# Attention, a Mish layer and a gated layer in one kernel: the written-out order planned anew with two times for each kind of transfer

## The chip, the core and the metric

The kernel runs on one core of a Trainium2 chip. The metric is the device time of one execution in microseconds. Three runs of the kernel before took 959.82, 963.29 and 963.5 us; the median is 963.29 us.

## What is computed

Inputs and outputs are float32. Three layers follow each other, on 4 batches of 576 tokens with 8 heads of 64 columns:

```python
# 1. attention, blocks of 64 tokens, a block sees itself and the blocks before it
scores = where(block_i >= block_j, (q @ k.T) / 8, -1e9)
attn = softmax(scores);  x = (attn @ v)            # 2304 tokens x 512
# 2. Mish layer, 512 -> 2048 -> 512
h = x @ w_in;  g = h * tanh(log1p(exp(min(h, 20))));  x = g @ w_out
# 3. RMS norm and gated layer, 512 -> 1536 -> 512
xn = x / sqrt(mean(x * x) + 1e-6) * rms_g
out = (silu(xn @ w_gate) * (xn @ w_val)) @ w_out2
```

## The kernel before, in words

**Arithmetic.** Most products are made of three float16 products of high and low halves ("hi" and "lo"), so each tile is first scaled and split by ScalarE, VectorE or GpSimd. The first 256 tokens go through the Mish layer in float32 (N32 = 1), and the first batch has float32 queries and keys (B32 = 1). Weights arrive as 64-bit words that VectorE turns into float32 in three instructions a tile (`to_f32`, L578, L586 and L606, where L606 is the last one).

**Tiling.** Attention goes batch by batch through five query tiles of 128 rows (the last has 64). For each head, or pair of heads, TensorE makes scores `s` (L978 to L1001), VectorE the row maximum `mx` (L1018), ScalarE the exponential `e` (L1043), and the probabilities are split and transposed into `pt`, in the first query tiles on TensorE (L1068, L1089), from the fifth query tile of batch 0 on by a DMA transpose (L1134). TensorE then multiplies `pt` by `v` into `x` (L1147, L1155), and VectorE scales that into `xfl` (L1187). The Mish layer takes tiles of 256 tokens: eight steps of `h` (L1369 in float32, L1378 in float16), then `y` (L1447, L1439). Its first step, called h0 here, needs the first two query tiles of batch 0 and the first quarter of w_in (`wis0`). The first `y` needs the sixteen tiles `wos0` to `wos15` of w_out, in that order. The gated layer (L1790, L1925) comes last.

**What sets the order.** Nothing is issued as it is written in the code. Each operation is recorded with an engine, a time in ns and its buffers; `Plan.place` then lays all operations out by list scheduling, forwards and backwards in turn, and keeps the shortest result. Then the keys of that result are shifted by two tables of numbers, `SHIFT` (by part) and `FINE` (by operation), and placed once more. The instructions are issued in the order of the planned starts. All transfers go through one queue on SyncE, in order, each waiting there for its source and its buffer. In `place` a transfer that starts at t lands in the queue's time as

```python
bus = end[i] = max(t + T_BUS, bus) + ns
```

**Fillers.** In the first 60 us of the plan, each planned idle stretch of TensorE is filled with small products that nobody reads (`with_idle`, L1979, `shared<-idle_in,ones_h`): 75% of the stretch, 56 ns for each. They are instructions like any other: TensorE runs all of them before it takes up the next.

Of the kernel before, what the change touches and what calls it, by code (L numbers as in the profile page):

```python
# [24 lines left out]
PE, ACT, DVE, POOL, DMA, NONE = "PE", "ACT", "DVE", "POOL", "DMA", "NONE"  # L25
# [10 lines left out]
T_DGE, T_DGE_HEADS, T_BUS = 660.0, 720.0, 1250.0  # L36
# [7 lines left out]
class Shared(float):  # L44

    pass

# [43 lines left out]
class Plan:  # L91
# [46 lines left out]
    def place(self, key, back=False):  # L138
# [3 lines left out]
        n = len(ops)  # L142
        free = {e: 0.0 for e in (PE, ACT, DVE, POOL, DMA, NONE)}
        warm, win, busy, bus = True, 0, 0.0, 0.0
# [17 lines left out]
        while left:  # L162
# [65 lines left out]
            if e == DMA:  # L228
                free[e] = t + o.issue
                bus = end[i] = max(t + T_BUS, bus) + ns  # L230
# [92 lines left out]
def t_rows(n, nbytes):  # L323

    return n * {256: 12.0, 2048: 6.44, 4096: 13.44}[nbytes]
# [3 lines left out]
def block_attention_mish_mlp_gated_mlp(  # L329
# [13 lines left out]
    nc = tc.nc  # L343
# [447 lines left out]
    def split_k(b, a, pace):  # L791
# [6 lines left out]
        for tt in range(NTT):  # L798
# [9 lines left out]
                DMA, 1540.0 * n / P,  # L808
# [57 lines left out]
    def prep_q(b, tt, at):  # L866
# [15 lines left out]
        else:  # L882
# [13 lines left out]
            DMA, 1540.0 * n / P,  # L896
# [4 lines left out]
        op(DMA, 400, lambda: nc.sync.dma_start(out=w()[0:D, :, :n], in_=a()[D:P, :, :n]), r=[a], w=[(w, 0)], at=at)  # L901
        op(DMA, 400, lambda: nc.sync.dma_start(out=w()[D:P, :, :n], in_=a()[0:D, :, :n]), r=[a], w=[(w, 1)], at=at)
# [40 lines left out]
    def attention(b, i, at, pace):  # L943
# [113 lines left out]
        def probs(keys, es, at):  # L1057
# [50 lines left out]
            for z, e in enumerate(es):  # L1108
# [24 lines left out]
                DMA, 1.5 * wd,  # L1133
# [35 lines left out]
        def norm_x(half, xt, at):  # L1169
# [56 lines left out]
            if last:  # L1226
                for hh in range(2):
                    for s_ in range(2):
                        op(
                            DMA, 400,  # L1230
# [15 lines left out]
            for t, c0, jl, w in runs:  # L1246
                if t not in x16:
                    x16[t] = buf("m1", [P, 2 * NCC, T1], F16, f"x16_{t}", "x16", X_BUFS)
                op(
                    DMA, 770.0 * w,  # L1250
# [26 lines left out]
    op(DMA, 800, lambda: nc.sync.dma_start(out=rgb(), in_=rms_g.partition_broadcast(P)), w=[rgb], at=60000)  # L1277
# [183 lines left out]
    def norm(t, m, at):  # L1461
# [37 lines left out]
        def halves(pool, o0, o1, c0, part):  # L1499
# [4 lines left out]
            else:  # L1504
# [16 lines left out]
                DMA, {2: 824, 3: 1250}[w],  # L1521
# [225 lines left out]
    def load_xn(l, at):  # L1747
# [4 lines left out]
        for part, c0, c1 in ((0, 0, 2 * DM), (1, 2 * DM, 4 * DM), (2, 4 * DM, 7 * DM)):  # L1752
            for m in range(NM):
                r0 = (p * NM + m) * P
                op(
                    DMA, 1.5 * (c1 - c0),
# [154 lines left out]
    def mlp2_o(l, pps):  # L1911
# [4 lines left out]
        for z in range(2 * NM):  # L1916
# [30 lines left out]
            if fq == NQ2 - 1:  # L1947
                r0 = (p * 2 * NM + z) * P
                op(
                    DMA, t_rows(P, 2048), lambda x=x, r0=r0: nc.sync.dma_start(out=out[r0 : r0 + P, :], in_=x()),  # L1950
                    r=[x], at=a,
                )
# [35 lines left out]
ROUNDS = 10  # L1988
URGENT, URGE, ROUNDS2 = 3000.0, 50000.0, 0
SHIFT = {  # L1990
# [208 lines left out]
```

## Time and profile before

| | |
|---|---|
| median of 3 runs | 963.29 us (959.82 to 963.5) |
| the profiled execution | 958.27 us, of which the span shown is 956.5 us |
| TensorE, VectorE, ScalarE, GpSimd busy | 932.2, 785.3, 600.5, 509.9 us |
| transfers | 125.37 MB, mean 131 GB/s |
| mean granted clock of TensorE | 0.999 |

The profiled execution lies 1.77 us above its span and 5.02 us under the median. TensorE is busy nearly throughout, so a gain can only come from fillers, from its waits, or from the few microseconds before its first and after its last product. The busy time counts fillers as work, and a product of it is pipelined: the time of one in the profile is longer than the distance to the next, so a wait shorter than that overlap isn't seen as idle time.

### The profile page before, as it was taken

To read this page: it belongs to the slowest core of one execution; us is meant where nothing else is said; L and a number is where in the kernel's file an instruction comes from. 1 tells how busy PE (TensorE), PEld (TensorE's weight loads), DVE (VectorE), ACT (ScalarE), POOL (GpSimd) and SP (SyncE) were. 2 spreads that over 40 slices of the span, in tenths; PEclk is the share of its full clock that TensorE was granted. 3 is DMA by queue.
4 is the path that set the end of the run, shared out by engine and by line. 5 is a ranking of instruction groups with operands and counts; after the bars stand their busy time and mean duration, and the time that the engine had idled before them with its cause. 6 is when DMAs were issued, how large, how long until landed. Compare 5 with 4: busy or idle time off the path is not lost. (4 is left out here: it accounts for less than half of the span.)

```text
span 956.5 us, 18899 instructions
## 1 busy us (share of the span) xinstructions
PE 932.2 (97%) x6754; PEld 585.3 (61%) x6755; DVE 785.3 (82%) x1797; ACT 600.5 (63%) x1244; POOL 509.9 (53%) x659
## 2 busy tenths in 40 slices
PE   8999999899999999999999999999999999999998
PEld 7785566466666758666675665555555555545553
DVE  5999978987896689988884999899989989765654
ACT  4769679998699889887775654647454635312320
POOL 1249245885562447577551936768555856412321
PEclk9999999999999999999999999999999999999999
DMA  9754698699875498788663747755658270552002
GB/s 228 217 199 129 187 159 151 125 153 174 141 143 101 86 178 167 134 180 154 149 144 57 144 127 138 172 133 94 156 126 141 75 148 15 103 110 73 12 34 88
DMA packets 317183, 125.37 MB, mean 131 GB/s; under 512 B 296353, under 2 KB 296353, under 8 KB 317089
## 3 DMA queue, kind: packets, MB, share of 16 engines
q1 hardware_dynamic: 317088, 124.17, 61.4%
q8 instruction: 53, 0.87, 0.4%
q14 instruction: 42, 0.34, 0.1%
HBM read 50.07 MB, written 12.98 MB: 66 GB/s over the span
## 5 line engine op out<-in xcount | busy, mean ns | idle before, releaser
L1378 PE MATMUL h<-x,w1i 128*128 128x256 f16 x1536 | 179.3, 273 | 1.3 <-ACT f L1404 1.3
L1439 PE MATMUL y<-w1o,g 128*128 128x512 f16 x768 | 178.5, 379 | 1.8 <-DVE w1o L551 1.7
L1378 PEld LDWEIGHTS <-w1i 128*128 128x128 f16 x1536 | 146.3, 98 | 23.1 <-issue 2.7
L1790 PE MATMUL g<-xnT,w2g 128*128 128x384 f16 x756 | 129.0, 326 | 0.0
L1790 PE MATMUL v<-xnT,w2v 128*128 128x384 f16 x756 | 126.9, 326 | 0.0
L1439 PEld LDWEIGHTS <-g 128*128 128x128 f16 x768 | 71.1, 98 | 80.5 <-issue 5.1
L1790 PEld LDWEIGHTS <-w2g 128*128 128x128 f16 x756 | 73.8, 98 | 51.5 <-issue 0.4
L1790 PEld LDWEIGHTS <-w2v 128*128 128x128 f16 x756 | 74.0, 98 | 50.3
L1018 DVE TENSOR_REDUCE mx<-s 128x1 f32<-128x512 f32 (+4 forms) x128 | 70.1, 557 | 19.7 <-PE s L984 17.8
L1043 ACT ACTIVATE e<-s,bias,cS 128x512 f32<-128x512 f32 (+4 forms) x120 | 72.5, 607 | 21.0 <-POOL bias L1027 11.0
L1421 DVE SCALAR_TENSOR_TENSOR g<-f,ich,g 128x512 f16<-128x512 f32 x64 | 55.4, 871 | 10.7 <-ACT g L1416 6.6
L1155 PEld LDWEIGHTS <-pt 128*128 128x128 f16 x1128 | 48.7, 98 | 22.2 <-DMA pt<-p 8.2
L1155 PE MATMUL x<-v,pt 128*128 128x64 f16 (+1 forms) x1128 | 55.5, 199 | 4.2 <-DMA pt<-p 3.4
L518 POOL TENSOR_SCALAR p<-e 128x128 f16<-128x128 f32 (+2 forms) x57 | 27.0, 474 | 57.7 <-ACT e L1043 39.6
L1124 POOL TENSOR_TENSOR p<-e,p 128x512 f16<-128x512 f32 (+4 forms) x54 | 50.4, 937 | 6.5 <-DVE p L1117 2.9
L1043 ACT ACT_TABLE_LOAD x38 | 48.8, 1283 | 4.6 <-DVE bias L1027 3.9
L1404 ACT ACTIVATE f<-h,ch 128x512 f32<-128x512 f32 x64 | 43.4, 684 | 10.4 <-PE h L1378 8.6
L1404 ACT ACT_TABLE_LOAD x38 | 48.8, 1283 | 1.1 <-issue 0.4
L1828 POOL TENSOR_TENSOR p5g<-u2g,p5g 128x384 f32<-128x384 f32 x15 | 15.9, 1058 | 58.3 <-DVE sl22g L1828 54.6
L1124 DVE TENSOR_TENSOR p<-e,p 128x384 f16<-128x384 f32 (+4 forms) x58 | 37.6, 650 | 8.4 <-ACT p L1120 4.9
L983 PE MATMUL s<-kT,qT 128*128 128x384 f16 (+3 forms) x96 | 27.5, 299 | 6.1 <-ACT e L1043 5.9
L1808 ACT ACTIVATE p5v<-v,ck 128x384 f32<-128x384 f32 x18 | 10.4, 580 | 36.5 <-PE v L1790 36.5
(612 smaller groups left out, 2155.5 us busy)
## 6 DMA issues: line engine op xcount, KB each, us to landing
wir<-in_moe_w_in_dram SPq DMA_DIRECT2D x16, 512.0 KB, 5.1
wor<-in_moe_w_out_dram SPq DMA_DIRECT2D x16, 512.0 KB, 3.9
w2rg<-in_moe_w_gate_dram SPq DMA_DIRECT2D x24, 256.0 KB, 3.4
w2rv<-in_moe_w_val_dram SPq DMA_DIRECT2D x24, 256.0 KB, 3.0
w2ro<-in_moe_w_out_dram SPq DMA_DIRECT2D x24, 256.0 KB, 3.4
q<-in_q_dram SPq DMA_DIRECT2D x16, 256.0 KB, 3.8
k<-in_k_dram SPq DMA_DIRECT2D x16, 256.0 KB, 4.1
v<-in_v_dram SPq DMA_DIRECT2D x15, 256.0 KB, 4.4
```

Of the source, the lines that this page charges most:

```text
L518: nc.gpsimd.tensor_scalar(out=out_, in0=in_, scalar1=by, scalar2=1.0, op0=ALU.mult, op1=ALU.mult)
L983: nc.tensor.matmul(t, src[b, i]()[:, h, :], kT[b]()[:, h, 0:n], start=(ph == 0), stop=False)
L1018: lambda z=z, cols=cols: nc.vector.reduce_max(out=mx()[:, cols], in_=ts[z](), axis=AX.X),
L1043: lambda y=y, z=z, c0=c0, w=w, acc=acc, e=e, h=h: nc.scalar.activation(out=e()[:, c0 : c0 + w], in_=ts[z]()[:, y, :], func=AF.Exp, bias=bi ...
L1124: lo = lambda eng, z=z, ev=ev: eng.tensor_tensor(out=view(p16)[:, z, :, 1, :], in0=ev(0, kt), in1=view(p16)[:, z, :, 0, :], op=ALU.subtract)
L1155: nc.tensor.matmul(xt()[:, cols, :], pv(z)[:, t, ph, :], v16[b, t]()[:, vh, key * w : key * w + w], start=(t == 0 and y == 0), stop=(t == ...
L1378: nc.tensor.matmul(ph()[:, g, :], w1i[fq]()[:, cc, wh, f * P : (f + 1) * P], x()[:, xh * NCC + cc, :], start=(z == 0), stop=(z == 3 * NCC ...
L1404: ACT, t_act(W, 1, True), lambda: nc.scalar.activation(out=e(), in_=phf(), func=AF.Mish, scale=cs()),
L1421: lambda: nc.vector.scalar_tensor_tensor(out=g16()[:, 1], in0=hv(), scalar=sc(), in1=g16()[:, 0], op0=ALU.mult, op1=ALU.subtract),
L1439: nc.tensor.matmul(yps[t, m](), g16()[:, gh, g, m * P : (m + 1) * P], w1o[f]()[:, wh, :], start=(f == 0 and z == 0), stop=(f == NF1 - 1 an ...
L1790: nc.tensor.matmul(b(), w()[:, wo, wh, cc, :], x()[:, (2 * xo + xh) * 2 + cc, :], start=(i == 0), stop=(i == 5),)
L1828: f = lambda eng: eng.tensor_tensor(out=d(), in0=u(), in1=v(), op=ALU.add)
```

## The change

A transfer has two times now. `Moved` carries both: the one for a transfer by itself, and `queued`, the one behind another in the queue. The second is what the queue is held for; the difference is a delay of that transfer alone. Every kind of transfer gets a pair of numbers, the planner tries 20 rounds in place of 10, and both tables are new. No operation is added or taken away, and each works on the same data; what differs is the order on every engine, which of the allowed engines some operations run on, and the number of fillers.

```diff
+class Moved(float):
+    def __new__(cls, ns, queued):
+        x = float.__new__(cls, ns)
+        x.queued = queued
+        return x
...
-                bus = end[i] = max(t + T_BUS, bus) + ns
+                bus = end[i] = max(t + T_BUS + ns - ns.queued, bus) + ns.queued
...
-    return n * {256: 12.0, 2048: 6.44, 4096: 13.44}[nbytes]
+    return Moved(*(n * x for x in {256: (12.0, 9.2), 2048: (6.44, 6.3), 4096: (13.44, 11.4)}[nbytes]))
...  kT, qT: transposes of keys and queries
-                DMA, 1540.0 * n / P,
+                DMA, Moved(1330.0 * n / P, 1120.0 * n / P),
...  pt: transposed probabilities
-                DMA, 1.5 * wd,
+                DMA, Moved(1.3 * wd - 60.0, 1.1 * wd),
...  xn_d: the second layer's result to HBM
-                DMA, {2: 824, 3: 1250}[w],
+                DMA, {2: Moved(200.0, 620.0), 3: Moved(650.0, 900.0)}[w],
...  xnT: read back and transposed
-                    DMA, 1.5 * (c1 - c0),
+                    DMA, Moved(1850.0, 1380.0) if part < 2 else Moved(2300.0, 1800.0),
...
-ROUNDS = 10
+ROUNDS = 20
...
-    "": 503996, "q0_0": -2461588, "k0_0": -1320023, "k0_1": -610386, "k0_2": -1295851, "k0_3": -335452,
+    "": 1349539, "q0_0": -897928, "k0_0": -825919, "k0_1": -361070, "k0_2": -147912, "k0_3": -146826,
```

The same pairs of edits, left out here, stand at the copies qS (400 to 300 and 400), the copies into x16n (400 to 200 and 300), the transposes into x16 (770 a block to 880 and 700, or 1300 and 1150 for two), rms_g (800 to 800 and 1000) and the stores of the output (824 to 200 and 620).

**TensorE, second half of query tile 1 (batch 0), before.** `x0_1` is that tile's result for the first heads, `sqv` the norm of v, `tpqT_0_2` the transposed query tile 2, `tpp0_1_1` transposed probabilities of two heads of tile 1. Under the first "..." stand 15 more fillers, under the second 62, under the third 11.

```order
L1147 MATMUL x0_1_78_555<-v0_1_12_256,pt_0_1_0_546 128x64
L1979 LDWEIGHTS ones_h_111
L1979 MATMUL shared_131<-idle_in_113,ones_h_111 128x128
...
L492 MATMUL shared_131<-sqv_9_90,ones_h_111 128x5
...
L857 MATMUL tpqT_0_2_695<-ident_98,q0_2_62_353 128x128 x4
...
L1068 MATMUL tpp0_1_1_721<-ident_98,e0_1_1_445 128x128 x2
L1068 MATMUL tpp0_1_1_721<-ident_98,e0_1_3_516 128x128 x2
```

The same place now:

```order
L866 MATMUL tpqT_0_2_470<-ident_100,q0_2_62_284 128x128 x4
L1156 MATMUL x0_1_78_451<-spares_179,pt_0_1_0_438 128x64
L1156 MATMUL x0_1_78_451<-v0_1_12_217,pt_0_1_0_438 128x64
L501 LDWEIGHTS ones_h_111
L501 MATMUL shared_131<-sqv_9_90,ones_h_111 128x5
...
L631 MATMUL wiq0_396<-junk26_479,ones_h_111 128x512
...
L1077 MATMUL tpp0_1_1_502<-ident_100,e0_1_1_425 128x128 x2
L1077 MATMUL tpp0_1_1_502<-ident_100,e0_1_3_440 128x128 x2
```

Query tile 2 is transposed before the norm of v, and six fillers (two and four) stand where 90 stood. Up to h0, TensorE has 377 products before and 233 now: 241 fillers against 100, and three sums of squares of w_in (`wiq`, L622) that stand behind h0 now; all else is the same. Another 14 fillers stand behind h0.

**SyncE's queue, the same stretch, before.** `wir` are raw tiles of w_in, `k1` keys of batch 1.

```order
L750 DMA v0_2_14_281<-in_v_dram 128x8x64
L750 DMA v0_3_16_284<-in_v_dram 128x8x64
L750 DMA k1_0_64_302<-in_k_dram 128x8x64
L750 DMA k1_1_66_309<-in_k_dram 128x8x64
L566 DMA wir1_0_344<-in_moe_w_in_dram 128x1024
L750 DMA q0_2_62_353<-in_q_dram 128x8x64
```

And now:

```order
L759 DMA v0_4_18_240<-in_v_dram 64x8x64
L575 DMA wir0_2_250<-in_moe_w_in_dram 128x1024
L759 DMA v0_3_16_268<-in_v_dram 128x8x64
L759 DMA q0_2_62_284<-in_q_dram 128x8x64
L575 DMA wir0_3_301<-in_moe_w_in_dram 128x1024
L759 DMA k1_0_64_314<-in_k_dram 128x8x64
```

The load of query tile 2 is the 16th transfer in place of the 21st, ahead of the keys of batch 1.

**VectorE, before the last result that h0 needs (`xfl0_1_1`), before.** `v16` are split tiles of v, `wis` converted tiles of w_in.

```order
L551 SCALAR_TENSOR_TENSOR v16_0_0_615<-spares_188,sv0_607,v16_0_0_615 128x512
L606 SCALAR_TENSOR_TENSOR wis1_0_629<-wir1_0_344,wis1_0_629 128x512
L578 TENSOR_SCALAR wis1_1_737<-wir1_1_424 128x512
L1187 TENSOR_TENSOR xfl0_1_0_752<-x0_1_78_555,r_80_542 128x256
L578 TENSOR_SCALAR wis1_2_759<-wir1_2_482 128x512
...
L606 SCALAR_TENSOR_TENSOR wis1_2_759<-wir1_2_482,wis1_2_759 128x512
L578 TENSOR_SCALAR wis1_3_815<-wir1_3_508 128x512
L1187 TENSOR_TENSOR xfl0_1_1_828<-x0_1_81_780,r_83_796 128x256
```

And now:

```order
L1081 COPY pt_0_1_5_599<-tpp0_1_5_586 128x256
L587 TENSOR_SCALAR wis1_0_605<-wir1_0_372 128x512
L662 TENSOR_REDUCE wc_28_611<-wiq0_396 128x1
L595 SCALAR_TENSOR_TENSOR wis1_0_605<-wir1_0_372,wis1_0_605 128x512
L1196 TENSOR_TENSOR xfl0_1_1_625<-x0_1_81_572,r_83_570 128x256
L615 SCALAR_TENSOR_TENSOR wis1_0_605<-wir1_0_372,wis1_0_605 128x512
L587 TENSOR_SCALAR wis1_1_632<-wir1_1_434 128x512
```

Ahead of `xfl0_1_1` stood 89 instructions of VectorE and stand 66: the five L551 and the L546 that split v are behind it now, as are three L578, two L586 and three L606; nine copies of `pt` are ahead of it in place of six.

## Rows read from the trace of the kernel before

**Rows 1.** The page, busy time by engine: us, share of the span, instructions
```profile
PE 932.2 (97%) x6754; PEld 585.3 (61%) x6755; DVE 785.3 (82%) x1797; ACT 600.5 (63%) x1244; POOL 509.9 (53%) x659
```

**Rows 2.** Five stages: length, busy us by engine, granted clock, DMA share, GB/s
```profile
0.00:47.00 47.00, 43.87 (x421) 35.83 (x422) 33.13 (x94) 28.02 (x83) 8.50 (x25) 1.00 0.89 223
47.00:113.00 66.00, 65.77 (x337) 43.69 (x339) 62.18 (x122) 49.05 (x110) 36.64 (x37) 1.00 0.58 185
113.00:300.00 187.00, 175.98 (x1570) 116.59 (x1567) 158.21 (x462) 159.39 (x338) 110.71 (x170) 1.00 0.80 143
300.00:500.00 200.00, 195.13 (x1821) 136.89 (x1819) 168.00 (x446) 160.01 (x306) 120.83 (x188) 1.00 0.74 144
500.00:956.50 456.50, 451.41 (x2613) 252.30 (x2611) 363.76 (x676) 204.04 (x410) 233.26 (x241) 1.00 0.47 103
```

**Rows 3.** The fillers on TensorE: count | busy us, mean ns | idle
```profile
L1979 PE MATMUL shared<-idle_in,ones_h 128*128 128x128 bf16 x241 | 19.6, 232 | 2.2 <-DVE idle_in L439 1.9 <-DVE p2c L494 0.3
```

**Rows 4.** Timeline of TensorE, 30 to 48 us: start, us, instruction
```profile
32.07 3.68 PE L1979 MATMUL shared<-idle_in,ones_h 128*128 128x128 bf16 x63 [0.28 <-DVE p2c L494]
35.58 0.61 PE L857 MATMUL tpqT<-ident,q 128*128 128x128 f32 x4
...
36.64 0.61 PE L1068 MATMUL tpp<-ident,e 128*128 128x128 f32 x4
...
46.85 0.39 PE L622 MATMUL wiq<-junk,ones_h 128*128 128x512 bf16 x1
47.08 1.24 PE L1369 MATMUL h<-x,wis 128*128 128x256 f32 x5
```

**Rows 5.** Timeline of SyncE, the load of the query tile: start, issue time
```profile
24.47 0.39 SPq L750 DMA_DIRECT2D q<-in_q_dram  x1
```

**Rows 6.** All query tiles: from issue to landing
```profile
DMA to landing us min/median/max: 2.8/3.6/5.9
```

**Rows 7.** Timeline of ScalarE: an exponential of the second query tile
```profile
28.14 0.47 ACT L1043 ACTIVATE e<-s,bias 128x256 f32<-128x256 f32 x1
```

**Rows 8.** Groups on VectorE, 0 to 47 us, columns as above
```profile
L606 DVE SCALAR_TENSOR_TENSOR wis<-wir,wis 128x512 uint32<-128x512 uint32 x8 | 5.5, 683 | 0.1
L586 DVE SCALAR_TENSOR_TENSOR wis<-wir,wis 128x512 uint32<-128x512 uint32 x8 | 5.4, 682 | 0.1
L578 DVE TENSOR_SCALAR wis<-wir 128x512 uint32<-128x512 uint32 x8 | 3.8, 479 | 0.0
L551 DVE SCALAR_TENSOR_TENSOR v<-v,sv,v 128x512 f16<-128x512 f32 (+1 forms) x4 | 3.1, 818 | 0.0
...
L546 DVE TENSOR_SCALAR v<-v,sv 128x512 f16<-128x512 f32 x1 | 0.5, 485 | 0.0
```

**Rows 9.** Timeline of TensorE, up to the sixth tile of w_out
```profile
90.55 0.55 PE L1089 MATMUL tpp<-ident,e 128*128 128x128 f32 x3
90.94 0.42 PE L1155 MATMUL x<-v,pt 128*128 128x64 f16 x9
91.20 1.96 PE L1447 MATMUL y<-wos,spares 128*128 128x512 f32 x4
...
93.50 1.12 PE L978 MATMUL s<-kT,qT 64*128 64x512 f32 x2
94.46 0.19 PE L984 MATMUL s<-mask_col,mask_row 64*128 64x64 bf16 x1
94.71 0.70 PE L1447 MATMUL y<-wos,spares 128*128 128x512 f32 x1
```

**Rows 10.** Timeline of VectorE: last instruction that converts that tile
```profile
93.98 0.68 DVE L606 SCALAR_TENSOR_TENSOR wos<-wor,wos 128x512 uint32<-128x512 uint32 x1
```

**Rows 11.** Who TensorE waited for: total us, times, longest
```profile
PE s L983 <- ACT e L1043: 5.9, 10, 1.7
PE x L1155 <- DMA pt<-p: 3.4, 7, 0.9
```

**Rows 12.** All transposed probabilities: from issue to landing
```profile
DMA to landing us min/median/max: 2.4/3.3/5.2
```

More of the change, by code (lines that the diff above doesn't have):

```diff
@@ L895, in prep_q @@
         op(
-            DMA, 1540.0 * n / P,
+            DMA, Moved(1330.0 * n / P, 1120.0 * n / P),
             lambda: nc.sync.dma_start_transpose(out=a()[:, :, :n], in_=x()[:n]),
@@ L900, in prep_q @@
         w = buf("at", [P, H, P], F16, f"qS_{b}_{tt}", "qS", 2)
-        op(DMA, 400, lambda: nc.sync.dma_start(out=w()[0:D, :, :n], in_=a()[D:P, :, :n]), r=[a], w=[(w, 0)], at=at)
-        op(DMA, 400, lambda: nc.sync.dma_start(out=w()[D:P, :, :n], in_=a()[0:D, :, :n]), r=[a], w=[(w, 1)], at=at)
+        op(DMA, Moved(300.0, 400.0), lambda: nc.sync.dma_start(out=w()[0:D, :, :n], in_=a()[D:P, :, :n]), r=[a], w=[(w, 0)], at=at)
+        op(DMA, Moved(300.0, 400.0), lambda: nc.sync.dma_start(out=w()[D:P, :, :n], in_=a()[0:D, :, :n]), r=[a], w=[(w, 1)], at=at)
         qT[b, tt], qS[b, tt] = a, w
@@ L1229, in norm_x @@
                         op(
-                            DMA, 400,
+                            DMA, Moved(200.0, 300.0),
                             lambda hh=hh, s_=s_: nc.sync.dma_start(
@@ L1249, in norm_x @@
                 op(
-                    DMA, 770.0 * w,
+                    DMA, Moved(880.0 if w == 1 else 1300.0, 700.0 if w == 1 else 1150.0),
                     lambda t=t, c0=c0, jl=jl, w=w: nc.sync.dma_start_transpose(
@@ L1276, in block_attention_mish_mlp_gated_mlp @@
     rgb = keep("rgb", DM)
-    op(DMA, 800, lambda: nc.sync.dma_start(out=rgb(), in_=rms_g.partition_broadcast(P)), w=[rgb], at=60000)
+    op(DMA, Moved(800.0, 1000.0), lambda: nc.sync.dma_start(out=rgb(), in_=rms_g.partition_broadcast(P)), w=[rgb], at=60000)
     a_ = 70000
@@ L1949, in mlp2_o @@
                 op(
-                    DMA, t_rows(P, 2048), lambda x=x, r0=r0: nc.sync.dma_start(out=out[r0 : r0 + P, :], in_=x()),
+                    DMA, Moved(200.0, 620.0), lambda x=x, r0=r0: nc.sync.dma_start(out=out[r0 : r0 + P, :], in_=x()),
                     r=[x], at=a,
```

307 rows, old and new, of tables (FINE, SHIFT) are left out of this document.

## The prediction

> **What bounds the kernel now.** I read the page's busy times first. TensorE is busy 97% of the span, VectorE 82%, the other two under 65% [rows 1]. The second view is the table of five stages [rows 2]: the reader is to see where TensorE is not busy. In the last stage (500 us on) it idles 456.5 - 451.4 = 5.1 us in almost half of the run, so a new order finds little there. From 113 to 500 us it idles 11.0 + 4.9 = 15.9 us; from 47 to 113 us 0.2 us, and VectorE beside it is busy 62.2 of 66; in the first 47 us 3.1 us. That last figure hides something, since fillers count as work: 241 of them [rows 3]. The busy time of that group, 19.6 us, is too long for what they cost, as products overlap. The timeline gives the distance: 63 fillers run from 32.07 to 35.58, when the next product starts, so one costs 3.51 / 63 = 0.056 us [rows 4], and 241 cost 13.4 us. No real product of the kernel is added or dropped. So this change can win only from fillers (13.4 us), from waits in attention (up to 15.9 us) and from the edges, and it can lose in the same places.
>
> Were these fillers standing where TensorE had to wait anyway? The 63 of them stand ahead of the transposes of query tile 2. Its load was issued at 24.47 [rows 5], and no load of a query tile took over 5.9 us to land [rows 6], so it was there by 30.4; TensorE took it up at 35.58. At least 5.2 us of that filling was pure delay. The products behind (probabilities of tile 1) tell the same: their exponentials ran at 28.14 + 0.47 = 28.6 [rows 7], and TensorE reached them at 36.64 [rows 4].
>
> **The change part by part.**
>
> *First term, the front.* The new order has 141 fillers fewer ahead of h0: 141 x 0.056 = 7.9 us. Three sums of squares go behind h0; one takes 47.08 - 46.85 = 0.23 us to the next start [rows 4], so 0.7 us. TensorE's work up to h0, which starts at 47.08, shrinks by 8.6 us, and h0 would start at 38.5. Does anything else hold it there? Query tile 2 is 16th in the queue instead of 21st, so it does not come later. VectorE must finish `xfl0_1_1` first: ahead of it, five L551 at 0.82, one L546 (I take the 0.48 of L578), three L578 at 0.48, two L586 at 0.68 and three L606 at 0.68 are gone [rows 8], 4.1 + 0.5 + 1.4 + 1.4 + 2.0 = 9.4 us; at most five copies more come in, 2.4 us if each is as long as an L578. That is 7.0 us less of VectorE's 33.1 us up to 47 us [rows 2], 26 us of work before 38.5. So VectorE's sum does not hold h0, though a chain of waits can. Bounds: -5.2 us, the delay that is proven, to -8.6 us. I take -8.5, near the count, because nothing in the front is as full as TensorE, the transfers excepted (0.89 [rows 2]), whose order now has the query ahead of keys that nobody needs yet.
>
> *Second term, what is given back from 47 to 113 us.* Here VectorE converts the sixteen `wos` tiles, and TensorE uses each almost at once: the sixth is ready at 93.98 + 0.68 = 94.66 [rows 10], and its first `y` starts at 94.71 [rows 9], 0.05 us later. If h0 starts 8.5 us sooner and VectorE doesn't, `y` waits. What softens it is that the new order puts more of TensorE's other work between h0 and this `y`: 223 products for 166. By the distances of rows 9: one score pair more, 93.50 to 94.46, 0.96 us; 7 transposes at 0.39 / 3, 0.9 us; 27 products of `x` at 0.26 / 9, 0.8 us; then 14 fillers, 0.8 us, the three sums of squares, 0.7 us, and the half tile of query transposes, at most the 0.61 us of a whole one [rows 4]. Together about 4.5 us of cover (0.3 us less than the sum, the half tile counting half). VectorE's list up to this conversion is hardly shorter, 177 instructions for 180. With VectorE as late as before, 4.5 of the 8.5 us are kept; with VectorE ahead by 4 us, which its 13.9 idle us in the front [rows 2] would allow, all of it; with VectorE later by 4.5 us (the five L551 that it has pushed behind h0 cost 4.1), nothing. I take 5.5 kept, a little above the unmoved case, as earlier inputs let VectorE start part of its list earlier. Give-back +3.0, bounds 0 to +8.5.
>
> *Third term, attention from 113 to 500 us.* The transposed probabilities are planned as shorter transfers (at 512 columns, queued, 563 ns for 768; alone 606), so the planner dares to put the product with v nearer to its scores. I counted TensorE's work between a head's last score and its first `x` in both orders, with distances like those of rows 4 and 9: of 88 heads with a DMA transpose 11 had under 10 us of such cover and 23 have it now; the mean falls from 15.0 to 12.9 us. In the trace TensorE waited for such a transfer 7 times, 3.4 us in all, 0.9 us at the longest, and for an exponential ahead of a score 10 times, 5.9 us in all [rows 11]. The transfers land in 2.4 to 5.2 us, median 3.3 [rows 12], so two microseconds less of cover is no small part of it. Bounds: -3.4 us, if every wait for `pt` goes; +10.8 us, if twelve more heads wait the longest time seen (12 x 0.9). By the nearest row, 7 waits of 0.49 us in mean, 12 more heads of which one in three waits would cost 2 us, and the waits for exponentials can lose as much, being of the planner's making too. I take 0.
>
> *The last stage.* 5.1 us idle, of which the new order can neither lose nor win much: TensorE has work that is ready there. I take 0, and +-1 us.
>
> The sum: -8.5 + 3.0 + 0 + 0 = -5.5 us. The profiled execution took 958.27, so it would be 952.8. The median of the three runs stands 5.02 us higher, and the forecast for a median is 963.29 - 5.5 = 957.8 us.
>
> A rule that speaks against taking fillers out: the granted clock is 1.00 in all five stages [rows 2], the 2.4 GHz level, the first stage with its 241 fillers included. The Trainium skill ("TensorE: Matmul & The Clock Gate", section "What's actually happening") says that the default state is the throttled one and that activity releases it. By the row the fillers are only a cost; by the rule they may be what keeps the front at the high level. No run here shows TensorE at the low one, so the rule stays a rival.
>
> **The rivals.**
>
> *Deeper.* All of the front's gain is kept in part three too: VectorE comes earlier, and the waits for `pt` go. -8.5 - 3.4 = -11.9 us: 951.4. For it: transfers planned nearer to what they take; VectorE's idle time in the front. Against: VectorE at 62.2 of 66 right behind it, and the shorter covers. Chance 0.20.
>
> *VectorE takes it all.* The slack of 0.05 us [rows 9, 10] is no accident, the whole chain of `wos` runs at VectorE's pace, and VectorE reaches it no sooner: the front's gain comes back as waits ahead of `y`. 963 us, +-2. Against: the 4.5 us of added cover. Chance 0.22. That would also be the case in which the change does not do what it says: the order is another, the time is not.
>
> *Slower: covers too short.* In attention the product with v is placed so near that heads wait for `pt` as a rule. It decides once the 12 heads with newly short cover lose more than 5.5 / 12 = 0.46 us each; at 1.1 us each, between the longest `pt` wait (0.9) and the longest wait for an exponential (1.7) [rows 11], it is 13.2 - 5.5 = +7.7: 971 us. For it: cover shortened in 12 of 88 heads, and a queue busy 0.80 and 0.74 of the time [rows 2]. Against: eleven heads had short cover before and seven short waits came of it. Chance 0.18.
>
> *Slower: the clock.* With 141 fillers fewer the front drops to the 1.2 GHz level. Its real work, 43.9 - 13.4 = 30.5 us [rows 2 to 4], would at most double: +30.5 - 5.5, 988 us; if half of the stretch is touched, 973. Against: other products stand in the front throughout. Chance 0.04.
>
> **How the numbers follow.** The forecast has 0.36, with its own range of 953 to 961 (bounds of the second term, and two microseconds of the third). The range that should hold the time reaches over the deeper case (951, and 4 us for a front or a last stage that gives more) and into the slower one: 947 to 969. What this kernel's measurement can tell from no change is about 0.5%, 958.5 to 968.1. Faster than that: the deeper case and six tenths of the forecast, 0.20 + 0.22 = 0.42. Within: the rest of the forecast, 0.14, and nine tenths of VectorE's case, 0.20, and 0.02 of the covers' case, 0.36. Slower: 0.16 of the covers', 0.04 of the clock's and 0.02 of VectorE's, 0.22.
>
> **What would show it.** First term: h0 starts at 38 to 40 us; if at 42 or later, a wait in the front was behind the fillers, and its releaser will stand at the products ahead. Second: between h0 and the last `wos` tile, waits of `y` for L606 that sum to about 3 us, where there were none to speak of. Third: the waits of `x` for `pt` and of scores for exponentials sum to 9.3 us as before, give or take 3; at 20 the covers' case holds. The granted clock of the first stage stays at 1.00. Wrong I would be above all if the stretch from 113 to 500 us changed its length by more than the front did, in either direction, since I forecast it by count and not by row.

## The result, and the profile after

The changed kernel took 973.56 us (median of 4 runs, 973.11 to 974.59) beside 961.56 us for the kernel before in the same comparison: ratio 1.0131, 95% interval 1.0095 to 1.0167. It is 12 us slower where 5.5 us faster was forecast, and its whole interval lies above 1. Its profiled execution took 974.59 us, with a span of 972.8 us, 16.3 us more than before.

The page's busy times and the stages, columns as in [rows 1] and [rows 2]:

```profile
PE 934.8 (96%) x6628; PEld 579.5 (60%) x6628; DVE 776.9 (80%) x1790; ACT 600.4 (62%) x1249; POOL 499.8 (51%) x659
```
```profile
0.00:47.00 47.00, 44.75 (x322) 35.12 (x323) 32.04 (x85) 27.64 (x79) 8.70 (x28) 1.00 0.91 232
47.00:113.00 66.00, 61.38 (x326) 38.54 (x326) 58.23 (x123) 49.04 (x110) 34.73 (x36) 1.00 0.63 179
113.00:300.00 187.00, 174.86 (x1546) 115.37 (x1545) 155.32 (x452) 156.78 (x332) 116.75 (x181) 0.99 0.75 138
300.00:500.00 200.00, 187.17 (x1693) 126.36 (x1693) 155.27 (x428) 157.78 (x311) 111.61 (x171) 0.99 0.75 144
500.00:972.80 472.80, 466.63 (x2745) 264.11 (x2741) 376.06 (x706) 209.15 (x421) 227.98 (x244) 1.00 0.47 102
```

TensorE idles 4.6 us from 47 to 113 us, where it idled 0.2 [rows 2], and 12.8 us from 300 to 500 for 4.9. The waits of TensorE, columns as in [rows 11]; the line numbers are 9 higher in this kernel:

```profile
PE x L1164 <- DMA pt<-p: 9.9, 13, 1.9
PE s L992 <- ACT e L1052: 5.1, 10, 0.7
PE shared L501 <- ACT junk L771: 3.2, 4, 2.1
PE wiq L631 <- ACT junk L626: 3.1, 2, 2.3
PE h L1387 <- ACT f L1413: 2.9, 5, 1.0
```

Waits for transposed probabilities went from 3.4 to 9.9 us, and two kinds of wait that were small before grew: those of sums of squares for ScalarE's squares (`junk`), `shared` from 0.4 to 3.2 us and `wiq` from 0.2 to 3.1.

Busy time by stage doesn't tell where the 16.3 us arose, since the two orders do different work in a stage. So I added up, in both traces, the distance of each product of TensorE to the next (the lower typical one of its form, fillers left out), and compared the times at which both kernels had done the same sum; both end at about 887 us of such work. Each row rests on one profiled execution, and executions of one kernel can lie several microseconds apart (the kernel before took 956.90 to 964.23 us beside e1), so a step of one or two microseconds between rows says little. The differences to the kernel before, in us, for the runs of this document:

| work of TensorE done, us (time before) | 30 (52.9) | 60 (83.8) | 92 (115.8) | 110 (139.8) | 220 (268.2) | 320 (370.9) | 480 (543.6) | 880 (945.1) |
|---|---|---|---|---|---|---|---|---|
| changed kernel | -9.5 | -4.8 | -0.9 | +3.1 | +1.2 | +10.4 | +15.1 | +16.1 |
| e1, new until 268 us | -8.9 | -5.4 | -1.6 | +3.4 | +2.3 | +0.9 | +0.4 | +0.5 |
| e2, new from 268 to 530 us | +0.6 | +0.7 | +1.0 | +1.0 | +0.4 | +8.2 | +10.9 | +10.9 |
| e3, no fillers | +16.7 | +17.0 | +17.3 | +17.2 | +15.2 | +15.0 | +17.2 | +17.1 |
| f1, 90 fillers fewer | +6.8 | +6.7 | +6.7 | +5.9 | +4.4 | +5.3 | +6.0 | +5.9 |
| h1, another front until 115 us | -6.1 | -5.4 | -3.5 | -0.8 | -4.4 | -4.6 | -5.0 | -5.1 |

So the new front is 9.5 us ahead, all but 1 us of it is gone by 115 us, and from 268 us to the end of attention 14 us are lost. Behind that the two run alike. From 268 to 530 us TensorE was busy (the second row is the changed kernel's, columns as in [rows 2]):

```profile
268.00:530.00 262.00, 255.96 (x2279) 175.43 (x2278) 209.93 (x532) 208.75 (x403) 146.03 (x225) 1.00 0.70 135
268.00:530.00 262.00, 247.57 (x2213) 168.45 (x2212) 199.49 (x535) 204.94 (x392) 138.53 (x212) 0.99 0.70 133
```

That is 14.4 us of idle time in place of 6.0.

### The profile page after: what moved, and what is told of

It reads as the page before. It is cut to its first block, busy times and chain, and to the rows that moved or that the text cites. A ratio compares the mean times of both kernels' runs of the same rounds, so it can differ in the third digit from the quotient of the medians.

```text
span 972.8 us, 18609 instructions
## 1 busy us (share of the span) xinstructions
PE 934.8 (96%) x6628; PEld 579.5 (60%) x6628; DVE 776.9 (80%) x1790; ACT 600.4 (62%) x1249; POOL 499.8 (51%) x659
## 4 chain that ended last, share of the span: by engine, by line
PE 49%; DVE 14%; DMA 12%; ACT 10%; POOL 8%; issue 5%; SPq 3%; DVEq 0%; POOLq 0%; ACTq 0%
PE o L1934 12%; PE v L1799 10%; PE g L1799 9%; PE y L1448 6%; DMA pt<-p 6%; PE h L1387 4%; ACT e L1052 2%; ACT L1052 2%; PE s L987 2%; DVE mx L1027 1%; SPq L1766 1%; ACT L1413 1%; PE x L1164 1%; DMA wir<-in_moe_w_in_dram 1%; PE y L1456 1%
## 5 line engine op out<-in xcount | busy, mean ns | idle before, releaser
L1387 PE MATMUL h<-x,w1i 128*128 128x256 f16 x1536 | 182.4, 275 | 2.9 <-ACT f L1413 2.9
L1052 ACT ACTIVATE e<-s,bias,cS 128x512 f32<-128x512 f32 (+4 forms) x120 | 72.5, 607 | 23.0 <-DVE bias L1036 15.1
L1430 DVE SCALAR_TENSOR_TENSOR g<-f,ich,g 128x512 f16<-128x512 f32 x64 | 52.3, 820 | 16.0 <-ACT g L1425 14.6
L1133 POOL TENSOR_TENSOR p<-e,p 128x128 f16<-128x128 f32 (+4 forms) x52 | 47.2, 910 | 12.5 <-ACT p L1129 5.9
L1413 ACT ACTIVATE f<-h,ch 128x512 f32<-128x512 f32 x64 | 43.2, 682 | 10.4 <-PE h L1387 5.4
L1133 DVE TENSOR_TENSOR p<-e,p 128x384 f16<-128x384 f32 (+4 forms) x60 | 38.2, 640 | 8.2 <-POOL p L527 4.6
L1036 POOL TENSOR_SCALAR bias<-mx,nS 128x1 f32<-128x1 f32 (+1 forms) x40 | 21.8, 544 | 35.9 <-DVE mx L1027 21.2
```

The lines of the kernel that those rows point to most:

```text
L1052: lambda y=y, z=z, c0=c0, w=w, acc=acc, e=e, h=h: nc.scalar.activation(out=e()[:, c0 : c0 + w], in_=ts[z]()[:, y, :], func=AF.Exp, bias=bi ...
L1133: lo = lambda eng, z=z, ev=ev: eng.tensor_tensor(out=view(p16)[:, z, :, 1, :], in0=ev(0, kt), in1=view(p16)[:, z, :, 0, :], op=ALU.subtract)
L1387: nc.tensor.matmul(ph()[:, g, :], w1i[fq]()[:, cc, wh, f * P : (f + 1) * P], x()[:, xh * NCC + cc, :], start=(z == 0), stop=(z == 3 * NCC ...
L1413: ACT, t_act(W, 1, True), lambda: nc.scalar.activation(out=e(), in_=phf(), func=AF.Mish, scale=cs()),
L1430: lambda: nc.vector.scalar_tensor_tensor(out=g16()[:, 1], in0=hv(), scalar=sc(), in1=g16()[:, 0], op0=ALU.mult, op1=ALU.subtract),
```

## The experiments

All but e6 and e7 carry an order that was written out, so that nothing is planned anew and every other instruction stays where it was. Their code is the changed kernel's with this edit, and their line numbers are 31 lower than its own (x from `pt` is L1133, s L961, h L1356 and L1347):

```diff
-        rounds(key, ROUNDS)
...
+        for z, i in enumerate(ORDER):
+            o = self.ops[i]
+            o.start, o.pick = z, int(PICKS[i])
...
+            for _ in range(IDLES.get(o.idx, 0)):
+                self.idle()
```

ORDER, PICKS (the engine) and IDLES (fillers ahead of an operation) come from the plan of before ("old"), of after ("new"), or a joint of both.

**Where it is lost: e1 and e2.**

```diff
+ORDER = first 1544 of new, then the others as in old           # e1
+ORDER = first 1546 of old, new up to the 3036th, rest as old   # e2
```

> The order of the changed kernel for everything that the old order places before about 268 us (TensorE's work up to there is the same to 0.2 us), then the old order. Theory A, the loss sits in the stretch behind it (batches 2 and 3 of attention, where the new order fell from 1.3 us behind to 14 us behind): the run is 1 to 3 us above the kernel before, 961 to 966 us. Theory B, the new front leaves the other engines so far behind that whatever follows suffers: 8 to 12 us above, 969 to 974.

> The reverse: the old order up to the same point, the new order from there to the end of attention (about 530 us), then the old one. Theory A: the stretch loses by itself, 11 to 14 us above the kernel before, 972 to 976. Theory B: within 3 us of the kernel before. If transfers planned too short are the mechanism, the waits of x for pt sum to 6 us and more in this stretch, against some 2 in the kernel before.

e1: 959.08 us beside 958.37, ratio 0.9999 (0.9981 to 1.0017). e2: 968.66, ratio 1.0103 (1.0088 to 1.0118). Theory A holds in its substance: the stretch from 268 to 530 us loses by itself, 10.3 us in the medians where 11 to 14 were expected, and the new front neither gains nor harms. The waits of that stretch, first in the kernel before, then in the changed kernel, then in e2 (same columns):

```profile
PE s L983 <- ACT e L1043: 2.1, 5, 0.9
PE x L1155 <- DMA pt<-p: 1.7, 4, 0.6
```
```profile
PE x L1164 <- DMA pt<-p: 8.5, 9, 1.9
PE s L992 <- ACT e L1052: 2.5, 5, 0.7
```
```profile
PE x L1133 <- DMA pt<-p: 6.7, 9, 1.9
PE s L961 <- ACT e L1021: 2.6, 5, 0.7
PE shared L470 <- ACT junk L740: 1.7, 1, 1.7
```

**Fillers: e3 and f1.**

```diff
+IDLES = {}                                             # e3, with old ORDER
-IDLES = {..., 49: 16, 250: 63, 281: 11, ...}           # f1, with old ORDER
+IDLES = {...}
```

> The old order word for word, its 241 fillers left out. If fillers are only delay, h0 starts 8 to 13 us sooner than 47.1 us. Theory C, VectorE and ScalarE set the pace behind h0: by 113 us most of that is given back as waits of TensorE, and the time is 0 to 4 us below the kernel before, 958 to 962. Rival, it is kept: 950 to 954. Rival, the fillers held TensorE's clock up: a granted clock under 0.9 in the first 47 us and a time 3 us or more above.

> The old order word for word without the 90 fillers in the second half of query tile 1 (16, 63 and 11, between 30.7 and 36.6 us of the profile before; 151 stay). The first step of the prediction: h0 starts 4 to 6 us sooner than 47.1 us, and the granted clock and the distances stay at the high level. The second step as the runs so far have it: VectorE's chain of w_out gives nothing of it on, and the time is within 1.5 us of the kernel before. Rival, the gain is kept: 954 to 956. Rival, these fillers kept the clock up: products at double length in the 10 us behind, and 2 us or more above.

e3: 972.02 us, ratio 1.0146 (1.0123 to 1.0168). f1: 964.51 beside 960.29, ratio 1.0048 (1.0033 to 1.0062). In both the rival holds that the fillers kept the clock up; in f1, h0 started at 51.8 us and not at 41 to 43. Timeline of TensorE in f1 (start, us, instruction, idle before):

```profile
31.23 0.60 PE L1046 MATMUL tpp<-ident,e 128*128 128x128 f32 x4
31.67 0.44 PE L1957 MATMUL shared<-idle_in,ones_h 128*128 128x128 bf16 x5
35.20 0.47 PE L1125 MATMUL x<-spares,pt 128*128 128x64 f32 x2 [3.08 <-ACT pt L1053]
...
43.80 1.06 PE L1046 MATMUL tpp<-ident,e 128*128 128x128 f32 x4
...
51.78 3.62 PE L1347 MATMUL h<-x,wis 128*128 128x256 f32 x8
```

and its stages, columns as in [rows 2]:

```profile
0.00:34.00 34.00, 29.23 (x277) 24.09 (x277) 22.03 (x71) 19.88 (x58) 4.20 (x19) 1.00 0.97 241
34.00:38.00 4.00, 2.80 (x11) 2.28 (x12) 4.00 (x10) 2.90 (x11) 0.25 (x1) 0.68 0.65 149
38.00:42.00 4.00, 4.00 (x11) 1.68 (x9) 3.11 (x6) 1.65 (x5) 3.17 (x2) 0.50 0.81 211
42.00:47.00 5.00, 5.00 (x24) 4.32 (x23) 2.02 (x5) 2.04 (x7) 1.84 (x3) 0.50 0.71 204
47.00:56.00 9.00, 9.00 (x23) 5.40 (x23) 3.02 (x7) 4.53 (x11) 0.56 (x1) 0.50 0.21 63
56.00:60.00 4.00, 4.00 (x20) 3.53 (x19) 4.00 (x9) 0.60 (x1) 1.14 (x2) 1.00 0.17 23
```

With the 90 fillers gone TensorE waited 3.08 us for a copy of probabilities by ScalarE, and behind the wait the granted clock went to 0.50, the 1.2 GHz level, and stayed there to 56 us though TensorE was busy throughout: four transposes took 1.06 us instead of 0.60. By estimate that costs some 8 to 9 us: f1 is 6.8 us behind at 52.9 us, with 5.0 us of fillers less (90 x 0.056) and 3.1 us of wait more. e3 shows the same from the first product on:

```profile
4.27 1.09 PE L835 MATMUL tpqT<-ident,q 128*128 128x128 f32 x4 [4.27 <-DMA q<-in_q_dram]
...
40.50 1.09 PE L835 MATMUL tpqT<-ident,q 128*128 128x128 f32 x4
41.39 1.06 PE L1046 MATMUL tpp<-ident,e 128*128 128x128 f32 x4
```

beside 0.61 us for both in [rows 4]. Its granted clock reads 1.00 in the first 50 us, which the durations contradict: the first record of the clock in that trace stands at 65.9 us, and the column counts the time before it as full. The rival rule of the prediction (the Trainium skill, "TensorE: Matmul & The Clock Gate", "What's actually happening": throttled by default, released by activity) agrees with these two runs. The changed kernel kept the high level in its front with 100 fillers ahead of h0: TensorE's longest wait from 4 to 47 us was 0.2 us, and four transposes took 0.61 us there. f1 has more fillers (151), so their number alone does not decide.

**The dips in attention: e4.** In the changed kernel the clock fell twice, behind waits of 1.93 and 2.10 us. The table of windows around the second:

```profile
372.00:376.00 4.00, 1.90 (x19) 1.50 (x18) 2.75 (x9) 2.43 (x6) 3.81 (x7) 0.92 0.60 97
376.00:379.00 3.00, 3.00 (x16) 2.02 (x15) 2.89 (x9) 0.00 (x0) 2.92 (x3) 0.54 0.22 85
379.00:382.00 3.00, 3.00 (x24) 2.22 (x23) 2.92 (x16) 2.94 (x4) 1.35 (x2) 1.00 0.24 90
```

```diff
+IDLES = {..., 755: 30, 2009: 34}       # with new ORDER
```

> The new order word for word, with 30 and 34 products that nobody reads ahead of the two products for which TensorE waited 1.9 and 2.1 us (at 132.6 and 374.2 us of the profile after), behind which the granted clock stood at 0.50 for about 3.4 us each. Theory D, the wait pulls the clock down and each dip costs 1.7 us: the dips are gone and the time is 3 to 4 us below the changed kernel, 969.5 to 970.5. Rival, the dips cost nothing, as the next wait is as much shorter: no change from 973.5. If the fillers come out longer than the waits they cost up to 1 us.

974.77 us, ratio to before 1.0165 (1.0148 to 1.0182): nothing gained over 1.0131. The rival holds. The two dips are gone, and the 3 us came back as other waits (a third dip, as long, stood at 59 us behind a wait of 2.46 us; the granted clock was 0.97 from 47 to 113 us):

```profile
PE x L1133 <- DMA pt<-p: 15.3, 18, 1.7
PE s L961 <- DMA qS<-qT: 2.5, 2, 1.3
```

15.3 us of waits for `pt` instead of 9.9: in this stretch TensorE doesn't set the pace, and what it saves it waits. Two more figures say the same: the one of the changed kernel's four runs with a mean granted clock of 1.000 took 973.42 us, the others, at 0.996 to 0.998, 973.11 to 974.59; and s4 and s6 below lose 9 us from 268 us on without a dip there.

**Later use of the transfers: e5.** 87 operations get a later place.

```diff
+ORDER = new, with x (and what hangs on it) put behind what stands up to 1.0 us past pt's planned landing
```

> The new order, in which a product of x whose probabilities come by a transfer is put behind TensorE's other work until it stands at least 1.0 us behind the planned landing (87 operations move, 77 places of TensorE's list; all else, fillers too, as in the changed kernel). Theory A, transfers that are planned too short set TensorE's waits: the waits of x for pt fall from 9.9 us to under 5 and the time by 4 to 8 us below the changed kernel, 966 to 970. Rival E, the chains of the other engines (softmax to transfer and on to the next layer) set the pace and the wait only moves: pt waits fall, others rise, within 2 us of 973.5.

977.42 us, ratio 1.0174 (1.0143 to 1.0205). Theory A's gain of 4 to 8 us did not come. Rival E is nearer, though the time rose by 3.9 us where it allowed 2: the waits for `pt` fell, and the scores behind took them over.

```profile
PE s L961 <- ACT e L1021: 9.3, 16, 1.5
PE x L1133 <- DMA pt<-p: 6.0, 11, 2.1
```

**The planner's prices: e6, e7 and s1 to s7.** The two tables belong to the times that they were made for, so I compared orders that have no tables (e6, e7), and orders whose keys were searched at random, alike and as long, for several prices (s1 to s7). For s1 to s7 the edit below is that of the planner that made the order; the kernels that ran carry its ORDER, PICKS and IDLES alone.

```diff
-        if SHIFT:
+        if False:                               # e6 (old times, 20 rounds), e7 (pairs)
-T_DGE, T_DGE_HEADS, T_BUS = 660.0, 720.0, 1250.0
+T_DGE, T_DGE_HEADS, T_BUS = 660.0, 720.0, 1600.0       # s3; 1950.0 in s4 and s5
-                DMA, Moved(1.3 * wd - 60.0, 1.1 * wd),
+                DMA, Moved(1.5 * wd, 1.5 * wd),        # s6, s7; s1 old times, s2 pairs as they are
```

> The kernel before with its 20 rounds of planning (ROUNDS as in the change) and with neither table: the planner's own order by the old single times. It says nothing by itself: some 5 to 15 us above the kernel before, 965 to 975. It is the base of the next run.

> The changed kernel without the two tables: the planner's own order by the new pairs of times. Theory A, the pairs are too short for the chip: it is not faster than the run with the old times and no tables, and by up to 15 us slower, and x waits for pt by more than there. Rival F, the pairs are right and the new tables alone are bad: it is 5 us or more faster than the run with the old times, with no more waits for pt.

> A second order by the old single times: the planner's keys without tables, then a random search of the keys of 194,000 trials that keeps what makes the plan shorter; fillers by the same rule (230). The control for the next three, which are searched in the same way and as long. Theory A (the times decide): it comes out like the kernel before, 955 to 965 us. Theory G (the very order that somebody's search found decides, not the times): anything from 950 to 980.

> The same search with the new pairs of times (108 fillers). Theory A: like the changed kernel, 967 to 980 us, and 8 us or more slower than the run with the old times; the waits of x for pt sum to 9 us or more. Theory G: no rule, as likely faster than the old times' order as slower. If the granted clock of the first 47 us is under 0.95, part of the loss is the clock's and not the transfers'.

> The same search with the new pairs, every transfer landing 350 ns later (T_BUS 1250 to 1600), which is about what the traces of the changed kernel show in the mean beyond its plan; 150 fillers. Theory A: the loss is gone, 953 to 963 us, at least 8 us faster than the pairs as they are. Theory H, it is the pairs as such (a queue that is held too short a time) and not the landing: still 965 to 978.

> The same with 700 ns (T_BUS 1950), 151 fillers. Theory A with margin: 948 to 960, no slower than with 350 ns; the waits of x for pt under 4 us. If margin beyond the mean landing is worth nothing: 2 to 5 us slower than with 350 ns, as the plan is longer. Theory H: 965 to 978.

> The search with the new pairs and 700 ns more, from another seed (154 fillers). If the margin is what made the first such order 8 to 9 us faster than the pairs as they are: 958 to 970 us again, waits of x for pt under 5 us. If that was luck of one order: 970 or more.

> The same search with all new pairs but that of pt, which has its old single time (1.5 ns a column, alone or queued); 105 fillers. If the pair of pt alone carries the loss: 958 to 968 us, waits of x for pt as in the orders by the old times, 4 to 7 us. If all transfers share in it: 968 to 980, the waits for pt perhaps shorter, others longer.

> The same as the last from another seed (117 fillers), to see how far two orders by the same times lie apart: within 6 us of it.

The margin below is what the plan allows for a transfer from issue to use less what the trace shows from issue to landing, in the mean over all 477; the loss is the growth of the difference of the first table from 220 to 480 us of work, from the profiled execution alone. That was the fastest of four in s6 (967.29 of up to 973.36) and the slowest in s3 (979.50 of down to 973.72).

| order | ratio to before (95%) | margin, us | loss 268 to 543 us | waits for pt, us |
|---|---|---|---|---|
| before (old times) | 1 | 4.13 - 3.65 = +0.48 | 0 | 3.4 |
| s1, old times | 1.0081 (1.0061 to 1.0102) | +0.42 | 6.8 | 6.6 |
| s4, pairs + 700 ns | 1.0069 (1.0045 to 1.0093) | +0.37 | 8.8 | 3.7 |
| s5, pairs + 700 ns | 1.0068 (1.0041 to 1.0094) | +0.31 | 2.3 | 4.7 |
| s3, pairs + 350 ns | 1.0157 (1.0127 to 1.0187) | +0.04 | 12.6 | 9.4 |
| s6, pairs, old pt | 1.0105 (1.0070 to 1.0140) | -0.18 | 9.1 | 8.9 |
| s7, pairs, old pt | 1.0144 (1.0116 to 1.0171) | -0.19 | 9.0 | 6.8 |
| changed kernel (pairs) | 1.0131 (1.0095 to 1.0167) | 3.39 - 3.65 = -0.26 | 13.9 | 9.9 |
| s2, pairs | 1.0150 (1.0129 to 1.0171) | -0.31 | 9.6 | 8.4 |

Without tables the pairs were worse too: e6 1.0054 (1.0030 to 1.0078), e7 1.0243 (1.0201 to 1.0285); part of e7's is the clock, granted at 0.78 in its first 47 us. From 268 to 543 us, where no such dip stood, e7 lost 10.8 us and e6 5.1. Every order with a margin of 0.3 us or more lies at 1.0081 or below, every order with less at 1.0105 or above, though the intervals of the nearest two (s1 and s6) overlap, and nothing between +0.04 and +0.3 was tried. The margin goes with the price and hardly with the order, so these nine orders are five settings of the prices. A price that is right in the mean (s3) is no better than one that is too low: that part of theory A was wrong. By their numbers s1, s3 and s4 all came out slower than theory A allowed, and s3 and s4 lie in the range of H; but s4 and s5 are as fast as s1, the control by the old times, and faster than s2 with the same pairs, which speaks against H. Pricing `pt` alone as before is not enough (s6, s7). Two orders of one price differ by up to 8 us (before and s1), so theory G has a share: the old order is better than any that the search found, at the same price. The size of a single step in this table is not settled, and within the stretch from 268 us on the loss does not follow the margin (s4 8.8 us, s7 9.0); the division of the whole times is what nine orders show.

**Is a lead at the front worth anything: e8, h1, h2.**

```diff
+ORDER = first 616 of new, then the others as in old     # e8
+ORDER = first 636 of s4, then the others as in old      # h1
+ORDER = first 1543 of s6, then the others as in old     # h2
```

> The new order for what the old one places before about 115 us (TensorE's work up to there agrees to nothing, and it stood there 1.2 to 1.6 us ahead of the kernel before), then the old order. If what TensorE is ahead there is kept: 1 to 2 us below the kernel before. If the other engines are behind by as much: the same within 1 us. If the long wait of the new order at 132 us comes of the new front and not of the order behind it: 2 to 4 us above.

> The order searched with the pairs and 700 ns more (the first of the two) for what the old order places before about 115 us, then the old order. It stood 4.6 us ahead of the kernel before there. If the lead is kept: 4 us below the kernel before, 955. If the order behind it takes it back, as it did with the new order's front (5 us lost in the wait at 132 us): within 1 us of the kernel before or up to 1 us above.

> The order searched with the pairs and the old single time of pt for what the old order places before about 268 us, then the old order, which loses least from there on. It stood 3 us ahead there. If the lead is kept, and nothing is lost at the seam: 956 to 957, the fastest so far. If what is ahead there is TensorE alone: the same as the kernel before within 1 us.

e8: 961.22 beside 959.89, ratio 1.0014 (0.9994 to 1.0033): the lead is lost in the 25 us behind the joint, where TensorE waited 2.41 us for VectorE at 118.9 us and the granted clock was 0.54 from 119 to 126 us (1.00 in h1). h2: 967.98, ratio 1.0079 (1.0051 to 1.0107), a miss: TensorE waited 5.52 us at the joint for an exponential,

```profile
263.68 0.27 PE L961 MATMUL s<-kT,qT 128*128 128x128 f16 x1 [5.52 <-ACT e L1021]
```

so the other engines were not where the old order has them. h1: 956.88 beside 959.79, ratio 0.9963 (0.9941 to 0.9984): faster than both kernels, by 2.9 us in the medians against the kernel before, between the two expectations (its profiled execution, 953.42, was the fastest of its twelve, so the -5.1 of the first table flatters it). e8 stood 1.2 us ahead at the joint and h1 3.5. How far the other engines stood ahead in each was not measured; that e1's 9.5 us of lead came to nothing and h2's joint cost 5.5 us says that TensorE's place alone doesn't tell what a front is worth.

## Why the prediction was wrong

*First term, the front, -8.5 us.* Near in size, and a little beyond its bound of -8.6: h0 starts at 36.90 us (timeline of TensorE after),

```profile
36.46 0.61 PE L1988 MATMUL shared<-idle_in,ones_h 128*128 128x128 bf16 x8
36.90 1.95 PE L1378 MATMUL h<-x,wis 128*128 128x256 f32 x8
```

10.2 us sooner, 9.5 by equal work. Its reason was wrong. "At least 5.2 us of that filling was pure delay" holds for the transposes that stood next, which were ready, but not for TensorE: the `x` behind them was not ready. f1 takes out just these fillers, and the wait that they covered (3.1 us) appears, with the clock behind it. So the new order did not gain the time by dropping fillers alone; it also has other work in their place.

*Second term, 3.0 us given back.* The term was mis-sized: 8.6 us (from -9.5 to -0.9). The rival "VectorE takes it all" had the price right, 8.5. TensorE waited for sums of squares of w_in and for `wos`, and both end at VectorE's conversions: the square that `wiq` waited for 2.31 us had itself waited for `wis` (TensorE, then ScalarE after),

```profile
59.39 0.59 PE L631 MATMUL wiq<-junk,ones_h 128*128 128x512 bf16 x2 [2.31 <-ACT junk L626]
```
```profile
58.71 0.63 ACT L626 ACTIVATE junk<-wis 128x512 bf16<-128x512 f32 x1 [2.23 <-DVE wis L615]
```

and the sixth `wos` was converted at 94.87 + 1.14 = 96.01 us, later than the 94.66 of [rows 10], though the first `y` had started at 70.57 us instead of 79.07; its `y` waited 0.76 us (VectorE, then TensorE after):

```profile
94.87 1.14 DVE L615 SCALAR_TENSOR_TENSOR wos<-wor,wos 128x512 uint32<-128x512 uint32 x1
```
```profile
96.07 1.98 PE L1456 MATMUL y<-wos,spares 128*128 128x512 f32 x4 [0.76 <-DVE wos L615]
```

The forecast sign, waits of `y` of about 3 us, did not come: they sum to 0.8. The added cover of 4.5 us that I counted did not help, because the delays fell on other products ahead of it: by the distances of the first table, 3.4 us more than before ahead of `wiq`, 3 to 4 ahead of `s` (of which the profile shows only 0.5 as idle time) and 0.9 ahead of `y`. What made `s` late is open.

*Third term, attention, 0.* This is the step that failed: +16.0 us (from -0.9 at 116 us to +15.1 at 544), beyond its bound of +10.8, and more than the front gained, which the prediction named as its own sign of being wrong. The shorter cover was counted (23 heads under 10 us for 11) and then put at 2 us, set off against other waits. The bound priced each late head by its longest wait for `pt` before, 0.9 us. After, the longest is 1.9, and the waits from 268 to 530 us grew from 1.7 to 8.5 us, about half of the 14 us lost there; by the distances of the first table, 8 of the 14 us stand just ahead of products of `x`. The rival "covers too short" has this mechanism in part and came near the time (971), with some luck: 13 waits are not "as a rule" among 88 heads, its sign (waits for `pt` and exponentials of 20 us) did not come, they sum to 15.0 by the two lines of [rows 11], and it kept 5.5 us of the front.

What the runs add is the price. Not 12 heads but all transfers are planned to arrive, in the mean, 0.26 us sooner than they do, where the old times left 0.48 us to spare. Orders searched alike lost less when the price had such a margin (0.7 to 0.8% against 1.05 to 1.6%), so the price accounts for a part of the loss. The rest is open: s1, by the old price, loses 0.8% to the old order, e5 shows that later products of `x` alone don't cure it, and s4 lost 8.8 us in this stretch with a margin of +0.37 and only 3.7 us of waits for `pt`. That a late landing goes on through exponentials, sums and the next scores is my reading and not shown. The chain of waits after has places that fit it (start, us, what):

```profile
317.34 4.76 DMA pt<-p
...
352.01 4.16 DMA pt<-p
...
368.69 4.63 DMA v<-in_v_dram
373.40 0.73 ACT junk L771 x2
374.18 0.17 PE shared L501
```

The transfers themselves did not change. All of `pt` after:

```profile
DMA to landing us min/median/max: 2.4/3.4/5.7
```

against 2.4, 3.3 and 5.2 in [rows 12]. I weighed how long TensorE's cover was, and not that the old single times, too long by half a microsecond, had been a margin.

*Last stage.* As forecast: +1.0 us from 543 us on. *The clock rival* was placed in the front, where the changed kernel kept the high level; that its half case gave 973 is chance. The two dips in attention are real, and e4 shows that they cost nothing there. "No run here shows TensorE at the low one" misread the column of [rows 2]: in the kernel before, the first record of the clock stands at 6.2 us, and ahead of it four transposes took almost twice their later time (timeline of TensorE before):

```profile
4.19 1.06 PE L857 MATMUL tpqT<-ident,q 128*128 128x128 f32 x4
```

## What to carry to other kernels

A planner's price for a transfer is also its safety margin: before making prices truer, compare the planned with the traced landing and try a margin (here searched orders with 0.3 us and more in the mean lost 0.7 to 0.8% to the old order, and those with 0.04 us and less 1.05 to 1.6%). A new order competes with the old one as it stands: at the same prices a search lost 0.8% to it. A lead of the busiest engine in one stage may be worth nothing at the end: compare times at equal work, stage by stage, before counting it. Idle fillers may stand for a wait and hold the clock at once, so take them out one place at a time and read the clock behind it.

## What was not expected of the hardware

After one wait of 3.08 us, TensorE stayed at the 1.2 GHz level for 20 us (35.5 to 55.9 us in f1) though it was busy without a pause; after waits of 1.93 and 2.10 us in the changed kernel it came back within 4 us, and a wait of 2.31 us there (at 59.4 us) left it at the 2.4 GHz level. So the length of a wait alone did not tell what it does to the clock. Short dips cost nothing in the changed kernel, but in the kernel before they go with longer times: of its 66 executions beside these runs, the 29 with a mean granted clock of 1.000 took 959.0 us in the mean and the 7 with 0.997 or less 963.9; whether the clock or the waits ahead of it cost that is not shown. And the granted clock can read 1.00 while products take twice their time, as in the first 50 us of e3: compare a product's duration before trusting that column.
